# Attention and two expert stages on one core: the seven-product stage in four blocks of 384 tokens, TensorE operands placed by side of SBUF, begun at weight group 3

## The chip, the cores and the metric

The program runs on 1 core of one Trainium2 chip, and its other cores are idle. The metric is the device time of one execution in microseconds; a figure for the kernel is the median of its runs.

## The reference

The reference is a chain of three parts over B=2, H=8, S=768, D=64, that is 1,536 tokens of width 512. First comes windowed attention with block summaries, then a dense mixture of four experts (every expert works on every token), then a mixture of eight experts of which one or none is taken per token.

```python
x = attn_out.transpose(0, 2, 1, 3).reshape(B * S, H * D)   # 1536 x 512
p = domain_probs / (domain_probs.sum(-1, keepdims=True) + 1e-09)
for e in range(4):                                         # w1[e] 512x1024, w2[e] 1024x512
    h = np.maximum(x @ w1[e], 0.0)
    out += p[:, e:e + 1] * (h @ w2[e])
x = out
do_compute = x @ w_skip > 0
e_idx = argmax(x[do_compute] @ w_gate)                     # one of 8 experts
out[do_compute] = x + gate_w * (np.maximum(x @ w1[e], 0) @ w2[e])
```

The change touches the dense mixture above all. Its weights come in 16 groups: group g holds 256 of the 1,024 hidden columns of expert g // 4.

## The kernel before, in words

Every large product is made of three fp32r products of high and low parts: a value is copied to fp32r by ScalarE (`wh`, `xh`, `hh`), VectorE subtracts that from the value (`wl`, `xl`, `hl`), and TensorE forms h*h + h*l + l*h.

**Phase 1.** Groups 0 and 1 of the dense mixture run in blocks of two tiles (256 tokens) between the pieces of attention. As soon as attention is done, group 2 is loaded and split. **Plain groups.** Groups 2 and 3 run in `moe_block` with three blocks of 512 tokens. One chunk is half a group (128 hidden columns) for one block: `part_a` (line 363) makes 12 matmuls of 512 columns into one bank and then `hh` and `hl`; `part_b` (line 383) makes three matmuls of 512 columns per tile of 128 tokens with `w2`. In the order written out, the `part_b` of one chunk comes behind the `part_a` of the next.

**The seven-product stage.** `middle` takes groups 4 to 13. It multiplies `x` by `w1` of a group with seven products of half-size blocks in place of eight. The tokens are taken in pairs of blocks, here pair "l" (two blocks of 512 tokens) and pair "s" (two of 256). A product is a `burst` of six matmuls (line 509). Products 1, 2 and 3 use `x` itself, products 4 to 7 use sums of blocks of `x` (`xslh`, `xsll`, `xssh`, `xssl`), which `x_sums` makes once; products 3, 6 and 7 use sums of blocks of `w1` (`wsh`, `wsl`), which GpSimd makes per group (`sums`, lines 464 to 467) and ScalarE and VectorE split (`sum_parts`). Bursts accumulate in PSUM and are copied out between two of them: product 1 is copied from bank `ba` to `bb`, product 6 adds to `bb` and is copied out as `u2` (line 542), product 7 adds to `bb` and VectorE adds it to `s5` (line 551), product 4 adds to `bb` once more. `part` then makes `hh` and `hl` of a quarter of the hidden values. `second` (lines 570 and 572) multiplies them with `w2`, six matmuls of 512 columns for each tile, and VectorE adds the result into `acc`. A group has 42 burst matmuls of 512 columns, 42 of 256 and 72 of `second`. The order is a list (`order`), with one `second` after nearly every burst and the steps of the next group's weights (`w_steps`) at fixed places.

**Ends.** Groups 14 and 15 run in `moe_block` again, in blocks of 4, 3, 3 and 2 tiles, and the routing of each finished block (`route_block`) runs between the matmuls of the next one. The last block's routing runs beside the first slot ("x") of the routed mixture, whose rows are found from the first `NE` tiles alone. From `middle` on the order on every engine is as written; ahead of it a planner orders the instructions of each engine.

**Memory.** Tile pools grow from both ends of a partition. From the bottom: `ident`, `acc`, `pr`, `x` of tokens 512 to 1535, the buffers of `h`, the weight splits `w1`, `w2` of odd and even groups, `x` of tokens 0 to 511, the raw weights. From the top during `middle`: the pool `msum` (sums of `x`, sums of `w1`, `u2`, `s5`), and below it the pool `mh` (`hhl`, `hll`, `hhs`, `hls`). Added up from the tile sizes, all of the lower stack but the raw weights ends at byte 131,904, and `mh` and `msum` lie above byte 142,000.

Of the kernel before, what the change touches and what calls it, by code (L numbers as in the profile page):

```python
# [24 lines left out]
def attention_moe_kernel(  # L25
# [26 lines left out]
    acc = left.tile([P, NTILE, DM], F32, name="acc")  # L52
# [4 lines left out]
    xsplit = [None, [mp.tile([P, KC, NT - 4 * P], F32R, name=n) for n in ("xh1", "xl1")]]  # L57
# [5 lines left out]
    xsplit[0] = [xp.tile([P, KC, 4 * P], F32R, name=n) for n in ("xh0", "xl0")]  # L63
    wrp = xstack.enter_context(tc.tile_pool(name="wraw", bufs=1))

    def x_at(n0, n):

        i = int(n0 >= 4 * P)
        return [x[:, :, n0 - 4 * P * i : n0 - 4 * P * i + n] for x in xsplit[i]]


    wtiles = {}

    def w_parts(g, i):
        return [wps[g % 2].tile([P, KC * GF], F32R, name=f"w{i}{n}{g}", tag=f"w{i}{n}") for n in "hl"]

    def load_w(g):
        w1t = w_parts(g, 1)
# [13 lines left out]
        wtiles[g] = [raw, w1t, None]  # L92

    def split_w(g, i):
        if i > 1 and wtiles[g][2] is None:
            wtiles[g][2] = w_parts(g, 2)
        wh, wl = wtiles[g][1 + i // 2]
        w = KC * GF // 2
        s = slice(i % 2 * w, (i % 2 + 1) * w)
        r = wtiles[g][0][i // 2][:, s]  # L100
        (nc.gpsimd.tensor_copy if (g, i) in WPOOL else nc.scalar.copy)(wh[:, s], r)  # L101
        nc.vector.tensor_sub(wl[:, s], r, wh[:, s].bitcast(F32))  # L102
# [151 lines left out]
    def v_sum(b):  # L254
# [11 lines left out]
        vsum[b, "m"] = ap1.tile([WC, H * D + 8], F32, name=f"vsm{b}", tag="vsm")[:, : H * D]  # L266
# [77 lines left out]
    def moe_block(gs, t0, nt):  # L344
# [8 lines left out]
        def part_a(ci, c):  # L353
            g, cc = gs[ci // ncc], ci % ncc
            wh, wl = wtiles[g][1]
# [4 lines left out]
            f0 = c * GF + cc * P  # L360
# [6 lines left out]
            if c == KC - 1:  # L367
                hh = hp_.tile([P, 512], F32R, name=f"hh{g}_{t0}_{cc}", tag="hh")
                hl = hp_.tile([P, 512], F32R, name=f"hl{g}_{t0}_{cc}", tag="hl")
# [37 lines left out]
    SGROUPS = range(4, E1 * NG - 2)  # L407

    PAIRS = {"l": (4 * P, 4 * P), "s": (0, 2 * P)}
    xsum, scr = {}, {}  # L410

    def x_quarter(p, i, j, c=slice(0, 2)):

        n0, n = PAIRS[p]
        return [x[:, 2 * i + c.start : 2 * i + c.stop, :] for x in x_at(n0 + j * n, n)]

    def x_sums(pool):
# [3 lines left out]
        def unit(p, c):  # L421
            n = PAIRS[p][1]
            k = c.stop - c.start
            xt = {q: pool.tile([P, k, n], F32, name=f"x{q}{p}{c.start}", tag=f"x{q}") for q in ("11", "12", "21", "22")}
            ts = [pool.tile([P, k, n], F32, name=f"t{i}{p}{c.start}", tag=f"t{i}") for i in range(4)]
# [19 lines left out]
        for p, c in (("l", slice(0, 1)), ("l", slice(1, 2)), ("s", slice(0, 2))):  # L445
            us = []
            for i in range(12):
                def step(i=i, p=p, c=c, us=us):
                    if not us:
                        us.extend(unit(p, c))  # L450
                    us[i]()
                steps.append(step)
        return steps

    def w_steps(g):
# [3 lines left out]
        def sums():  # L459
            raw = wtiles[g][0][0].rearrange("p (c f) -> p c f", c=KC)  # L460
            a11, a12, a21, a22 = (raw[:, 2 * j : 2 * j + 2, i * P : (i + 1) * P] for i in range(2) for j in range(2))
            t = scr["w"].tile([P, 3, 2, P], F32, name=f"ws{g}", tag="ws")
# [5 lines left out]
            parts = [scr["w"].tile([P, 3, 2, P], F32R, name=f"ws{n}{g}", tag=f"ws{n}{g % 2}") for n in "hl"]  # L468
            wtiles[g] += [parts, t]

        def sum_parts(i):
            (h, l), t = wtiles[g][3:]
            s = slice(0, 2) if i == 0 else slice(2, 3)
            nc.scalar.copy(h[:, s], t[:, s])
            nc.vector.tensor_sub(l[:, s], t[:, s], h[:, s].bitcast(F32))  # L475
# [3 lines left out]
            lambda: load_w(g), sums if mid else no, lambda: split_w(g, 1), lambda: split_w(g, 0),  # L479
            (lambda: sum_parts(0)) if mid else no, (lambda: sum_parts(1)) if mid else no,  # L480
            lambda: split_w(g, 2), lambda: split_w(g, 3),
        ]

    def pair_work(g, p, state_):

        n0, n = PAIRS[p]
        w1h, w1l = wtiles[g][1]
        wsh, wsl = wtiles[g][3]
        e = g // NG
        ba, be, bb = (bank[i] for i in ((0, 6, 7) if p == "l" else (1, 6, 5)))  # L490
        hs, fs = {}, {}

        def wq(i, j):
            return [[w[:, (2 * j + c) * GF + i * P : (2 * j + c) * GF + (i + 1) * P] for w in (w1h, w1l)] for c in range(2)]

        def wsum(k):
            return [[w[:, k, c, :] for w in (wsh, wsl)] for c in range(2)]
# [16 lines left out]
        def tmp(nm):  # L514

            pad = 8 if nm + p == "s5s" else 0
            t = fs[nm] = scr["w"].tile([P, n + pad], F32, name=f"{nm}{p}{g}", tag=f"{nm}{p}")[:, :n]
            return t

        def part(i, j, src):  # L520
            if p == "l" and j == 1:
                pool, tag = hp_, ("hh", "hl")
            else:
                pool, tag = scr["h"], (f"hh{p}{i}{j}", f"hl{p}{i}{j}")
            hh, hl = (pool.tile([P, n], F32R, name=f"{t}_{p}{g}_{i}{j}", tag=t) for t in tag)
# [36 lines left out]
        def second(j, t):  # L562
            w2h, w2l = wtiles[g][2]
            b = bank[2 + state_["b"] % 3]
# [6 lines left out]
            t_ = n0 // P + j * (n // P) + t  # L571
# [7 lines left out]
    def middle(todo):  # L579

        todo = list(todo)
        state_ = dict(b=0)

        wh = wtiles[SGROUPS[0]][1][0]
        nc.tensor.matmul(bank[7], wh[:, :P], wh[:, :512], start=True, stop=True)
        at = {0: (0,), 2: (1,), 3: (2,), 5: (3,), 7: (4,), 9: (5,), 10: (6,), 12: (7,)}

        order = ("l1", "l5", "s1", "l6", "l3", "s6", "l7", "s5", "l2", "s7", "l4", "s3", "s2", "s4")
        for g in SGROUPS:
            nxt = w_steps(g + 1)  # L590
            work = {p: pair_work(g, p, state_) for p in PAIRS}
            for i, (p, k) in enumerate(order):
                work[p][0][k]()
                for k_ in at.get(i, ()):
                    nxt[k_]()
                if i == 10:
                    todo += work["l"][1][0]
                for _ in range(2 if g == SGROUPS[0] and i < 2 else i not in (9, 10)):
                    if todo:
                        todo.pop(0)()  # L600
            todo += work["l"][1][1] + work["s"][1][0] + work["s"][1][1]
        return todo
# [28 lines left out]
    NE = 7  # L631
# [650 lines left out]
    for g in range(2, SGROUPS[0]):  # L1282
        for i in range(3):
            moe_block((g,), 4 * i, 4)
    for gs, t0, n in (
        ((last - 1,), 0, 4), ((last,), 0, 4), ((last - 1,), 4, 3), ((last,), 4, 3),
        ((last - 1, last), 7, 3), ((last - 1, last), 10, 2),
    ):
        moe_block(gs, t0, n)
# [39 lines left out]
    for ch in chunks:  # L1329
# [13 lines left out]
        if ch["gs"] == (last - 1,) and first and ch["t0"] == 0:  # L1343
            ctx.enter_context(tc.manual_schedule())
            prev = dict(gs=(last - 2,), last=True, b=middle(prev["b"]))
            load_w(last)
        micros = list(ch["a"])
        if prev is not None:
            micros += prev["b"]
        for k_, f in enumerate(micros):  # L1350
# [6 lines left out]
            elif fin:  # L1357
                if ch["t0"] == 10 and ch["last"] and k_ == 1:
                    xt = slot_trans("x", early["xg"], bank[7])
                if ch["gs"] == (last - 1,) and ch["t0"] == 0 and k_ in (3, 6):  # L1360
                    split_w(last, 2 * ch["ci"] + k_ // 6)
                if ch["t0"] == 10 and ch["gs"][0] == last - 1 and micro_ % PRE == PRE - 1:
# [3 lines left out]
        if p1:  # L1366
            if ch["last"] and blk == len(PH1) - 1:
                run_to(len(alist))
                astack.close()
                scr["w"] = sstack.enter_context(tc.tile_pool(name="msum", bufs=1, side="right", reuse_waits="tile"))  # L1370
                for p_, (_, n_) in PAIRS.items():
                    xsum[p_] = [scr["w"].tile([P, 4, 2, n_], F32R, name=f"xs{p_}{q_}") for q_ in "hl"]
                xsteps = x_sums(tstack.enter_context(tc.tile_pool(name="mtmp", bufs=1, side="right", reuse_waits="tile")))
# [3 lines left out]
        elif not fin:  # L1377
# [7 lines left out]
            else:  # L1385
                if first and ch["t0"] == 0:
                    wsteps = w_steps(g + 1)
                for _ in range(1 + (len(wsteps) < 5)):
                    if wsteps:
                        wsteps.pop(0)()  # L1390
            for _ in range(3):
                xsteps.pop(0)()
            if not xsteps:
# [14 lines left out]
        if ch["gs"] == (last,) and ch["t0"] == 0 and ch["last"]:  # L1408
# [3 lines left out]
        if prev is not None and prev["gs"][-1] == last and prev["last"]:  # L1412
# [3 lines left out]
            if prev["t0"] == 4:  # L1416
                r += [None] * 3 + [early_list] + [None] * 3 + [early_gather, early_close]
            if prev["t0"] == 7:
# [45 lines left out]
    more_units(NTILE // 2 - 1, NTILE // 2)  # L1464
# [86 lines left out]
```

## Time and profile before

| | us |
|---|---|
| median of 3 runs | 700.65 |
| lowest and highest | 696.39 and 702.2 |
| the profiled execution | 699.05 |
| its span, first to last instruction | 697.3 |
| mean granted TensorE clock in it | 0.995 of full speed |

The profiled execution is 1.75 us longer than its span and 1.6 us shorter than the median. Times within a trace are counted from the start of the span. In a row of a group of instructions, "out<-in" names what is written and what is read; of a matmul the first name behind the arrow is the moving operand and the second the stationary one. Matmuls overlap in the records, so that the pace is read from start to start and not from the duration.

### The profile page before, as it was taken

The numbers are of one execution on the slowest core, as the hardware profiler recorded it, in microseconds if no ns is written. First come the engines' busy times: TensorE is split into PE (matmuls) and PEld (weight loads), VectorE is DVE, ScalarE is ACT, GpSimd is POOL, SyncE is SP. The second block draws the span as 40 slices with busy tenths as digits, with TensorE's granted clock in tenths as the row PEclk, the third lists the DMA queues.
The fourth block names the chain that finished last, engine by engine and source line by source line (L and its number), as shares of the span: only waits on it lengthen the run. The fifth ranks groups of instructions, "written<-read, shape, count | busy, mean of one in ns | idle before, by whom it ended". The sixth has DMA issues, their size and how long they took to land. (4 is left out here: it accounts for less than half of the span.)

```text
span 697.3 us, 10979 instructions
## 1 busy us (share of the span) xinstructions
PE 681.7 (98%) x4072; PEld 546.3 (78%) x4072; DVE 426.9 (61%) x1035; ACT 245.1 (35%) x617; POOL 103.4 (15%) x182
## 2 busy tenths in 40 slices
PE   6899999999999999999999999999999999999996
PEld 6788888788888888888888888888888888674361
DVE  5987664797537565665657465665653465694441
ACT  3766564432114232332323232232311223381250
POOL 5317200020101010101101010100010002331230
PEclk9999999999999999999999999999999999999999
DMA  8966210020000100000001100000050167668991
GB/s 240 258 208 162 65 47 24 31 91 31 31 0 31 61 31 31 31 31 30 31 31 37 54 31 31 31 31 30 31 213 0 62 259 300 211 221 317 413 410 53
DMA packets 39877, 73.78 MB, mean 106 GB/s; under 512 B 16740, under 2 KB 19812, under 8 KB 39824
## 3 DMA queue, kind: packets, MB, share of 16 engines
q1 hardware_dynamic: 38592, 70.31, 29.5%
q0 software_dynamic: 960, 2.25, 1.0%
q8 instruction: 32, 0.52, 0.3%
q10 hardware_dynamic: 272, 0.52, 0.2%
q14 instruction: 21, 0.17, 0.1%
HBM read 66.10 MB, written 7.86 MB: 106 GB/s over the span
## 5 line engine op out<-in xcount | busy, mean ns | idle before, releaser
L572 DVE SCALAR_TENSOR_TENSOR acc<-bank,pr,acc 128x512 f32<-128x512 f32 x120 | 89.4, 746 | 50.9 <-PE bank L570 50.2
L363 PE MATMUL bank<-xh,w1h 128*128 128x256 f32 (+2 forms) x208 | 68.5, 333 | 0.0
L363 PE MATMUL bank<-xl,w1h 128*128 128x256 f32 (+2 forms) x208 | 67.6, 326 | 0.0
L363 PE MATMUL bank<-xh,w1l 128*128 128x256 f32 (+2 forms) x208 | 67.4, 325 | 0.0
L383 PE MATMUL bank<-w2h,hh 128*128 128x512 f32 x144 | 58.4, 405 | 0.0
L464 POOL TENSOR_TENSOR ws<-raw 128x256 f32<-128x256 f32 x10 | 7.5, 750 | 332.6 <-DVE wsl L475 237.8
L383 PE MATMUL bank<-w2l,hh 128*128 128x512 f32 x144 | 56.5, 392 | 0.0
L370 ACT ACTIVATE hh<-bank 128x256 fp32r<-128x256 f32 (+2 forms) x52 | 24.1, 463 | 89.8 <-PE bank L363 83.5
L383 PE MATMUL bank<-w2h,hl 128*128 128x512 f32 x144 | 54.0, 398 | 1.6 <-DVE hl L371 1.6
L371 DVE SCALAR_TENSOR_TENSOR hl<-bank,hh 128x256 fp32r<-128x256 f32 (+2 forms) x52 | 27.0, 520 | 46.2 <-ACT hh L370 46.2
L295 ACT ACTIVATE sm<-sm,mn 128x120 f32<-128x120 f32 x96 | 36.7, 384 | 16.2 <-DVE mn L290 16.2
L363 PEld LDWEIGHTS bank<-xh,w1h 128*128 128x128 f32 x208 | 39.1, 189 | 4.2 <-DVE hl L371 0.4
L363 PEld LDWEIGHTS bank<-xl,w1h 128*128 128x128 f32 x208 | 39.4, 189 | 3.3
L363 PEld LDWEIGHTS bank<-xh,w1l 128*128 128x128 f32 x208 | 39.3, 189 | 2.5
L393 DVE SCALAR_TENSOR_TENSOR acc<-bank,pr,acc 128x512 f32<-128x512 f32 x43 | 29.8, 743 | 15.2 <-PE bank L383 15.2
L102 DVE TENSOR_TENSOR w1l<-raw,w1h 128x512 fp32r<-128x512 f32 x30 | 20.6, 690 | 22.4 <-ACT w1h L101 22.3
L383 PEld LDWEIGHTS bank<-w2h,hl 128*128 128x128 f32 x144 | 26.6, 188 | 8.7 <-DVE hl L371 3.3
L383 PEld LDWEIGHTS bank<-w2h,hh 128*128 128x128 f32 x144 | 27.2, 189 | 6.5 <-issue 2.3
L570 PE MATMUL bank<-w2h,hll_l 128*128 128x512 f32 x80 | 31.6, 395 | 0.0
L570 PE MATMUL bank<-w2l,hhl_l 128*128 128x512 f32 x80 | 31.6, 395 | 0.0
L570 PE MATMUL bank<-w2h,hhl_l 128*128 128x512 f32 x80 | 31.6, 395 | 0.0
L570 PE MATMUL bank<-w2h,hhs_s 128*128 128x512 f32 x80 | 31.6, 395 | 0.0
(357 smaller groups left out, 1741.1 us busy)
## 6 DMA issues: line engine op xcount, KB each, us to landing
raw<-in_moe_w_dram SPq DMA_DIRECT2D x30, 512.0 KB, 3.1
ra<-in_moe_w_dram SPq DMA_DIRECT2D x27, 512.0 KB, 9.8
rb<-in_moe_w_dram SPq DMA_DIRECT2D x21, 512.0 KB, 9.4
acc<-in_moe_w_dram SPq DMA_DIRECT2D x15, 512.0 KB, 10.1
vwin<-in_v_dram SPq DMA_DIRECT2D x24, 192.0 KB, 3.5
kt<-in_k_dram SPq DMA_DIRECT2D x8, 384.0 KB, 6.0
qbd<-in_q_dram SPq DMA_DIRECT2D x24, 128.0 KB, 4.0
out_dram<-xg SPq DMA_DIRECT2D x12, 256.0 KB, 3.0
```

The lines of the kernel that those rows point to most:

```text
L102: nc.vector.tensor_sub(wl[:, s], r, wh[:, s].bitcast(F32))
L295: nc.scalar.activation(sm[:, h, :], sm[:, h, :], AF.Exp, bias=mn[:, h : h + 1], scale=-1.0, accum_out=su[:, h : h + 1],)
L363: nc.tensor.matmul(b[:, :n], wt[:, f0 : f0 + P], xt[:, c, :], start=(c == 0 and i == 0), stop=(c == KC - 1 and i == 2),)
L370: nc.scalar.activation(hh[:, :n], b[:, :n], AF.Relu)
L371: nc.vector.scalar_tensor_tensor(out=hl[:, :n], in0=b[:, :n], scalar=0.0, in1=hh[:, :n].bitcast(F32), op0=ALU.max, op1=ALU.subtract,)
L383: nc.tensor.matmul(bank[2 + t], ht[:, t * P : (t + 1) * P], wt[:, f0 : f0 + DM], start=(ci == 0 and i == 0), stop=(ci == nch - 1 and i == 2),)
L393: nc.vector.scalar_tensor_tensor(out=a, in0=bank[2 + t], scalar=sc, in1=a, op0=ALU.mult, op1=ALU.add,)
L464: tt(out=t[:, 1], in0=a11, in1=a21, op=ALU.subtract)
L570: nc.tensor.matmul(b, a, w[:, s], start=i == 0 and k_ == 0, stop=i == 1 and k_ == 2)
L572: nc.vector.scalar_tensor_tensor(out=acc[:, t_, :], in0=b, scalar=pr[:, t_, e : e + 1], in1=acc[:, t_, :], op0=ALU.mult, op1=ALU.add,)
```

## The change

`acc` moves from the bottom of SBUF to its top. `x` is kept in two halves of 768 tokens. `w1` of a group is kept as two tiles, one for each half of the hidden columns. In the seven-product stage the second half of `w1` and two of the three sums of `w1` go to the upper pool `msum`, the third sum and the parts of two quarters of `h` to the pool `mh`, and the parts of the quarter (1, 1) to the room that the second half of `w1` leaves below. Added up from the tile sizes, the lower stack then ends at byte 113,472, `mh` lies between 113,600 and 129,984, and all operands of TensorE in `msum` lie above 133,000. Products 1, 2, 3 and `second` have both operands in the lower part, products 4 to 7 in the upper.

The pairs become "a" (tokens 0 to 767) and "b" (768 to 1535), each of two blocks of 384 tokens. The order of a group becomes: product 3 of the group before for a and b, load of the next weights, products 1a, 1b, the twelve `second` of the group before with most of the weight steps, 2a, 2b, 5a, 5b, 6a, 6b, 7a, 7b, 4a, 4b. The `hl` of a part is issued one step later than its `hh`. The stage begins at group 3. Group 2 and groups 14 and 15 run in blocks of three tiles, `NE` goes from 7 to 6, and the last block to be routed has three tiles in place of two. The sums of `x` start in the last block of phase 1, with the additions of high and low parts on GpSimd in place of VectorE.

```diff
-    acc = left.tile([P, NTILE, DM], F32, name="acc")
+    right = ctx.enter_context(tc.tile_pool(name="rows", bufs=1, side="right"))
+    acc = right.tile([P, NTILE * DM + 8], F32, name="acc")[:, : NTILE * DM].rearrange("p (t d) -> p t d", d=DM)
...
+    SGROUPS = range(3, E1 * NG - 2)
+    def w1_parts(g, i):
+        if i and g in SGROUPS:
+            return [scr["w"].tile([P, KC * P], F32R, name=f"w11{n}{g}", tag=f"w11{n}{g % 2}") for n in "hl"]
+        return [wps[g % 2].tile([P, KC * P], F32R, name=f"w1{i}{n}{g}", tag=f"w1{i}{n}") for n in "hl"]
...
-    PAIRS = {"l": (4 * P, 4 * P), "s": (0, 2 * P)}
+    TB = 3 * P
+    PAIRS = {"a": 0, "b": 2 * TB}
...
             def whole(i, j):
                 h, l = x_quarter(p, i, j, c)
-                nc.vector.tensor_add(xt[f"{i + 1}{j + 1}"], h.bitcast(F32), l.bitcast(F32))
+                nc.gpsimd.tensor_tensor(out=xt[f"{i + 1}{j + 1}"], in0=h.bitcast(F32), in1=l.bitcast(F32), op=ALU.add)
...
+            pool, s = (scr["w"], slice(0, 2)) if i == 0 else (scr["h"], slice(2, 3))
...
-        ba, be, bb = (bank[i] for i in ((0, 6, 7) if p == "l" else (1, 6, 5)))
+        ba, be, bb = (bank[i] for i in ((0, 4, 6) if p == "a" else (1, 5, 7)))
...
             nc.scalar.activation(hh, src, AF.Relu)
-            nc.vector.scalar_tensor_tensor(
+            state_["late"].append(lambda: nc.vector.scalar_tensor_tensor(
                 out=hl, in0=src, scalar=0.0, in1=hh.bitcast(F32), op0=ALU.max, op1=ALU.subtract,
-            )
+            ))
...
-            b = bank[2 + state_["b"] % 3]
+            b = bank[2 + state_["b"] % 4]
...
-        order = ("l1", "l5", "s1", "l6", "l3", "s6", "l7", "s5", "l2", "s7", "l4", "s3", "s2", "s4")
+        x = x_at(0, 4 * P)[0][:, 0, :]
+        for b in (bank[6], bank[7]):
+            nc.tensor.matmul(b, x[:, :P], x, start=True, stop=True)
+        def step(f):
+            late, state_["late"] = state_["late"], []
+            f()
+            for l in late:
+                l()
+        work = None
         for g in SGROUPS:
+            last_, work = work, {p: pair_work(g, p, state_) for p in PAIRS}
             nxt = w_steps(g + 1)
+            if last_:
+                step(last_["a"][0]["3"])
+                step(last_["b"][0]["3"])
+            nxt[0]()
+            step(work["a"][0]["1"])
+            step(work["b"][0]["1"])
+            if last_:
+                todo += [f for j in range(2) for p in PAIRS for f in last_[p][1][j]]
+            at = {1: 1, 2: 2, 5: 3, 7: 4, 9: 7}
+            for i, f in enumerate(todo):
+                step(f)
+                if i in at:
+                    nxt[at.pop(i)]()
+            for k in at.values():
+                nxt[k]()
+            todo = []
+            step(work["a"][0]["2"])
+            step(work["b"][0]["2"])
+            nxt[5]()
+            step(work["a"][0]["5"])
+            step(work["b"][0]["5"])
+            nxt[6]()
+            for k in "674":
+                for p in PAIRS:
+                    step(work[p][0][k])
...
-    NE = 7
+    NE = 6
...
-        for i in range(3):
-            moe_block((g,), 4 * i, 4)
+        for i in range(4):
+            moe_block((g,), 3 * i, 3)
-    for gs, t0, n in (
-        ((last - 1,), 0, 4), ((last,), 0, 4), ((last - 1,), 4, 3), ((last,), 4, 3),
-        ((last - 1, last), 7, 3), ((last - 1, last), 10, 2),
+    for gs, t0 in (
+        ((last - 1,), 0), ((last,), 0), ((last - 1,), 3), ((last,), 3), ((last - 1, last), 6), ((last - 1, last), 9),
     ):
```

## Rows read from the trace of the kernel before

**Rows 1.** The page, busy time of TensorE, its share of the span, instructions

```profile
PE 681.7 (98%) x4072; PEld 546.3 (78%) x4072; DVE 426.9 (61%) x1035; ACT 245.1 (35%) x617; POOL 103.4 (15%) x182
```

**Rows 2.** The waits of TensorE's matmuls: us in total, times, longest

```profile
PE bank L383 <- DVE hl L371: 1.6, 3, 0.9
```

**Rows 3.** Busy time by stretch, core 0: the plain groups, one seven-product group

```profile
139.18:205.11 65.93, 65.92 (x289) 53.91 (x288) 43.63 (x68) 16.25 (x29) 6.64 (x8) 1.00 0.11 40
...
246.00:277.35 31.35, 31.35 (x158) 26.40 (x157) 19.28 (x31) 9.66 (x20) 3.28 (x4) 1.00 0.10 34
```

**Rows 4.** TensorE in order of time, behind the stage: start, duration

```profile
533.89 0.39 PE L363 MATMUL bank<-xh,w1h 128*128 128x512 f32 x1
...
539.33 0.33 PE L363 MATMUL bank<-xh,w1h 128*128 128x384 f32 x1
...
541.43 0.39 PE L383 MATMUL bank<-w2h,hh 128*128 128x512 f32 x1
...
544.19 0.33 PE L363 MATMUL bank<-xh,w1h 128*128 128x384 f32 x1
...
573.94 0.33 PE L363 MATMUL bank<-xh,w1l 128*128 128x384 f32 x1
...
575.50 0.34 PE L363 MATMUL bank<-xh,w1l 128*128 128x384 f32 x1
```

**Rows 5.** TensorE in order of time, within the seven-product stage

```profile
380.94 0.39 PE L570 MATMUL bank<-w2h,hh_l 128*128 128x512 f32 x1
...
382.34 0.39 PE L509 MATMUL bank<-xh,w1h 128*128 128x512 f32 x1
...
383.71 0.39 PE L570 MATMUL bank<-w2h,hh_l 128*128 128x512 f32 x1
...
385.07 0.40 PE L509 MATMUL bank<-xslh,w1h 128*128 128x512 f32 x1
...
517.43 0.39 PE L570 MATMUL bank<-w2h,hhs_s 128*128 128x512 f32 x1
...
523.00 0.39 PE L363 MATMUL bank<-xh,w1h 128*128 128x512 f32 x1
```

**Rows 6.** The groups of instructions: busy us, mean ns | idle before

```profile
L101 ACT CAST w2h<-raw 128x512 fp32r<-128x512 f32 x29 | 17.4, 614 | 4.7 <-PE bank L383 3.8 <-DMA raw<-in_moe_w_dram 1.0
...
L466 POOL TENSOR_TENSOR ws<-raw 128x256 f32<-128x256 f32 x10 | 10.0, 1000 | 0.8
...
L464 POOL TENSOR_TENSOR ws<-raw 128x256 f32<-128x256 f32 x10 | 7.5, 750 | 332.6 <-DVE wsl L475 237.8 <-DMA raw<-in_moe_w_dram 94.8
```

**Rows 7.** Lines 542, 551, 527: duration ns min/median/max, first and last start

```profile
L542 ACT COPY u2l<-bank x10: 586/586/587, 211.8 to 485.6; 128x512 f32<-128x512 f32 x10
L542 ACT COPY u2s<-bank x10: 357/372/372, 214.8 to 490.6; 128x256 f32<-128x256 f32 x10
...
L551 DVE TENSOR_TENSOR s5l<-bank,s5l x10: 683/691/692, 216.3 to 493.3; 128x512 f32<-128x512 f32 x10
L551 DVE TENSOR_TENSOR s5s<-bank,s5s x10: 418/424/425, 219.8 to 500.3; 128x256 f32<-128x256 f32 x10
...
L527 DVE SCALAR_TENSOR_TENSOR hls_s<-u2s,hhs_s x10: 424/870/878, 223.6 to 504.4; 128x256 fp32r<-128x256 f32 x10
```

**Rows 8.** All engines in order of time at the end of a product 7

```profile
367.44 0.39 PE L509 MATMUL bank<-xslh,wsl 128*128 128x512 f32 x1
...
367.86 0.69 DVE L551 TENSOR_TENSOR s5l<-bank,s5l 128x512 f32<-128x512 f32 x1 [0.42 <-PE bank L509]
```

**Rows 9.** Busy time by stretch while the sums of x are made

```profile
128.00:163.00 35.00, 33.95 (x168) 27.69 (x168) 35.00 (x59) 15.45 (x30) 3.69 (x4) 1.00 0.17 61
```

**Rows 10.** In order of time, the last routing and the first gather behind it

```profile
610.53 0.22 DVE L749 CUSTOM_DVE_ANT_0 jk<-bank,oh,nin 128x8 f32<-128x8 f32 x1
...
612.67 1.04 POOL L1016 DMA_INDIRECT xg<-out_dram,ixb  x1 [1.79 <-DVE ixb L817]
...
616.18 0.61 PE L1030 MATMUL bank<-ident,xg 128*128 128x128 f32 x4
```

More of the change, by code (lines that the diff above doesn't have):

```diff
@@ L91, in load_w @@
         )
-        wtiles[g] = [raw, w1t, None]
+        wtiles[g] = [raw, [None, None], None]
     def split_w(g, i):
[L95 to L102, printed above, removed]
+        cp = nc.gpsimd.tensor_copy if (g, i) in WPOOL else nc.scalar.copy
+        if i < 2:
+            h, l = wtiles[g][1][i] = w1_parts(g, i)
+            r = wtiles[g][0][0].rearrange("p (c f) -> p c f", c=KC)[:, :, i * P : (i + 1) * P]
+            h, l = (t.rearrange("p (c f) -> p c f", c=KC) for t in (h, l))
+        else:
+            if wtiles[g][2] is None:
+                wtiles[g][2] = [wps[g % 2].tile([P, KC * GF], F32R, name=f"w2{n}{g}", tag=f"w2{n}") for n in "hl"]
+            sl = slice((i - 2) * DM, (i - 1) * DM)
+            h, l = (t[:, sl] for t in wtiles[g][2])
+            r = wtiles[g][0][1][:, sl]
+        cp(h, r)
+        nc.vector.tensor_sub(l, r, h.bitcast(F32))
     astack = ExitStack()
@@ L402, in moe_block @@
             ))
[L407 to L410 removed]
+    TB = 3 * P
+    PAIRS = {"a": 0, "b": 2 * TB}
     def x_quarter(p, i, j, c=slice(0, 2)):
[L414 to L415 removed]
+        return [x[:, 2 * i + c.start : 2 * i + c.stop, :] for x in x_at(PAIRS[p] + j * TB, TB)]
     def x_sums(pool):
@@ L443, in unit, with step @@
             ]
[L445 to L452, printed above, removed]
+        for p in PAIRS:
+            for c in (slice(0, 1), slice(1, 2)):
+                us = []
+                for i in range(12):
+                    def step(i=i, p=p, c=c, us=us):
+                        if not us:
+                            us.extend(unit(p, c))
+                        us[i]()
+                    steps.append(step)
         return steps
@@ L581, in middle @@
         todo = list(todo)
[L582 to L586, printed above, removed]
-        order = ("l1", "l5", "s1", "l6", "l3", "s6", "l7", "s5", "l2", "s7", "l4", "s3", "s2", "s4")
+        state_ = dict(b=0, late=[])
+        x = x_at(0, 4 * P)[0][:, 0, :]
+        for b in (bank[6], bank[7]):
+            nc.tensor.matmul(b, x[:, :P], x, start=True, stop=True)
@@ new lines, in middle @@
+            for k in at.values():
[8 more added lines that the diff above has]
+            for k in "674":
+                for p in PAIRS:
+                    step(work[p][0][k])
+        step(work["a"][0]["3"])
+        step(work["b"][0]["3"])
+        step(lambda: None)
+        return [f for j in range(2) for p in PAIRS for f in work[p][1][j]]
@@ L1346, in attention_moe_kernel @@
             load_w(last)
+        if p1 and first and blk == len(PH1) - 1:
+            run_to(len(alist))
+            astack.close()
+            scr["w"] = sstack.enter_context(tc.tile_pool(name="msum", bufs=1, side="right", reuse_waits="tile"))
+            scr["t"] = scr["w"].tile([P, 3, 2, P], F32, name="ws")
+            for p_ in PAIRS:
+                xsum[p_] = [scr["w"].tile([P, 4, 2, TB], F32R, name=f"xs{p_}{q_}") for q_ in "hl"]
+            xsteps = x_sums(tstack.enter_context(tc.tile_pool(name="mtmp", bufs=1, side="right", reuse_waits="tile")))
         micros = list(ch["a"])
@@ L1366, in attention_moe_kernel @@
         if p1:
+            if blk == len(PH1) - 1:
+                for _ in range(3):
+                    xsteps.pop(0)()
             if ch["last"] and blk == len(PH1) - 1:
[L1368 to L1373, printed above, removed]
                 load_w(2)
@@ L1387, in attention_moe_kernel @@
                     wsteps = w_steps(g + 1)
[L1388 to L1391, printed above, removed]
+                if wsteps:
+                    wsteps.pop(0)()
+            for _ in range(min(len(xsteps), 6)):
                 xsteps.pop(0)()
-            if not xsteps:
+            if not xsteps and "h" not in scr:
                 tstack.close()
@@ L1407, in attention_moe_kernel @@
                 free += [rap.tile([P, FF], F32, name=f"ra{i}") for i in range(NRA)]
-        if ch["gs"] == (last,) and ch["t0"] == 0 and ch["last"]:
+        if ch["gs"] == (last,) and ch["t0"] == 3 and ch["last"]:
             xstack.close()
```

104 lines of the change are left out of this document (46 added, 58 removed).

## The prediction

> **What bounds the kernel now.** I read the page first: TensorE is busy for 681.7 of 697.3 us [rows 1]. Then its waits: of the dense mixture only 1.6 us in three waits for an `hl` are left [rows 2]. The view by stretch says the same of the part that changes: in a seven-product group TensorE is busy for 31.35 of 31.35 us, VectorE for 19.28, ScalarE for 9.66, GpSimd for 3.28, at a granted clock of 1.00, the 2.4 GHz level [rows 3]. Nothing waits there, so the time is the number of matmuls times their pace, and the reader has to look at the pace from start to start. Behind the stage, where weights and moving operand both lie in the lower stack, 24 matmuls of 512 columns go from 533.89 to 539.33, 226.7 ns each, and nine of 384 go from 573.94 to 575.50, 173.3 ns each [rows 4]. Within the stage the pace depends on what is multiplied. A `second` with `hh_l` (lower stack) and `w2`, behind a product 1 of 512 columns, takes from 383.71 to 385.07 for its six, 226.7 ns each; but 24 matmuls of `second` with `hhs_s`, `hls_s` (above) and `w2` (below) go from 517.43 to 523.00, 232.1 ns each [rows 5]. So there is some 5 ns on a matmul of 512 columns whose operands lie on two sides. By the layout those are 18 burst matmuls and 48 of `second` in each group.
>
> **The change part by part.**
>
> *The ten groups 4 to 13.* A group keeps its 84 burst matmuls and 72 of `second`, and its burst columns: 42 x (512 + 256) = 84 x 384. With both operands on one side everywhere, as the sizes give it, a group is 84 x 173.3 + 72 x 226.7 ns = 14.56 + 16.32 = 30.88 us. To that come changes of size. Behind a change the pace is off for a while: twelve matmuls of 384 took 2.10 us in place of 2.08, the twelve of 512 behind them 2.76 in place of 2.72 [rows 4]; that is 0.06 us for there and back, once per group. A change of side at 384 columns is in no row; I bound it by nothing and by that 0.04 each and take 0.02, twice: 30.98 us. Against 31.35 that is 0.37 less, **3.7 us** for ten groups; with no cost of a change 4.7, with none of the gain 0.
>
> What hides the other engines' work there: copies and parts run while TensorE does the other pair's burst, 6 x 173.3 = 1.04 us. VectorE's addition began 0.42 us after the start of the last matmul of a product 7 [rows 8], some 0.2 after that matmul's share of 0.23 was over. At 384 columns it takes some 0.56 us and a copy by ScalarE 0.48 (between the rows for 256 and 512, [rows 7]), so a bank is free 0.7 to 0.76 us after its burst and wanted after 1.04. No wait, with 0.3 us to spare; without that cover each of four handovers (6 to 7 and 7 to 4, a and b) would cost what is missing. VectorE, ScalarE and GpSimd keep the amounts of [rows 3], far from the 31 us. I take nothing.
>
> *Group 3.* The two plain groups fill 65.93 us, 32.97 each [rows 3]; 32.97 to 30.98 is **2.0 us** less (1.6 at the old pace).
>
> *Entry of the stage.* In its first group only the last three `part_b` (9 x 226.7 = 2.04 us) stand where later twelve `second` do, and all weight steps of group 4 come at once, ahead of the Relus on ScalarE. With time counted from the start of 1a: two dummy matmuls and 1a, 1b end at 2.5, the copy of 1b at 3.2, the cast of `w1` at 3.8 (0.61 [rows 6]), its subtraction on VectorE at 4.5, GpSimd's four operations (0.75 to 1.0 each [rows 6], some 3.3) at 7.8. Then ScalarE has two casts of the sums, two Relus, two casts of `w2`, two copies of `s5` and that of `u2a`, 0.4 to 0.6 each, until about 12.2. TensorE wants to begin 7a at 2.5 + 2.04 + 6 x 1.04 = 10.8. I take a wait of **1.4 us**, once; 0 if the planner brings the weights earlier, 3 if GpSimd is slow. The second dummy is **0.2**. Behind TensorE nothing else is queued.
>
> *Group 2 and the ends.* Group 2 in four blocks is 96 x 173.3 + 72 x 226.7 = 32.96 us plus eight times 0.06, 33.4 against 32.97: **0.5 us** more. In groups 14 and 15 the columns and the count (192 of `part_a`) stay; four to eight chunks more change size: **0.3 us**.
>
> *The last routing.* The first gather starts at 612.67 and its rows are transposed at 616.18 [rows 10], 3.5 us later; I take it that TensorE has no slack there. With a third tile VectorE's chain of small operations ahead of the gather is longer by about a microsecond (an estimate: some six operations for each tile at the 0.22 us of one of them, [rows 10]), and TensorE's own steps for that tile, moved here from an earlier block, cover half: **0.5 us**, 0 to 1.5. The loads of the routed weights start a block of three tiles earlier and one 512 KB unit of `acc` comes free later; TensorE waits for none of them now. Nothing.
>
> *The sums of `x`.* VectorE is full from 128 to 163 us [rows 9], with 36 steps of x at about 0.69 [rows 7] among others; in 384 columns and without the additions it has 32 of about 0.56, 7 us less. They are needed some 30 us earlier than now, at the first 5a near 180 us, and GpSimd is idle there but for 6.64 us in 65.93 [rows 3]. Against that, VectorE has to wait for GpSimd's 16 additions of about 1 us. I take 0, from 1 us better (the waits of [rows 2] lie here) to 6 worse.
>
> *Sum.* -3.7 - 2.0 + 1.4 + 0.2 + 0.5 + 0.3 + 0.5 = -2.8 us, 699.05 to 696.25 for the profiled execution, which lies 1.6 under the median: **697.9 us** as a median. The three runs of before lie 5.8 us apart, and I count 1% (7 us) as what a measurement here can tell from no change.
>
> **The rivals.**
>
> *The side doesn't matter* (the change doesn't do what it says). The 5 ns could come from the alternation with bursts of 256 columns. For it speaks that a `second` with both operands below also takes 1.40 us between two bursts of 256 (380.94 to 382.34, [rows 5]); against it, that the 24 mixed ones in a row never come back to 226.7. Then eleven groups stay at 31.35 and the sum is -1.6 + 2.9 = +1.3: 702.0 us. The Trainium skill speaks for this rival: by "TensorE: Matmul & The Clock Gate", Part 2, step 1, TensorE reads moving operand and weights through two independent ports, and loading the next weights takes nothing from the running matmul. By that rule the time is this rival's; the 232.1 against 226.7 ns do not agree with it.
>
> *Slower: the sums of `x` come late.* Place: group 2, where VectorE's queue holds `total` and `low` behind GpSimd's additions and the `hl` of `part_a` behind those; `part_b` then waits for `hl`, as it did in [rows 2]. For it: a VectorE subtraction with two inputs in SBUF took 0.87 us in the median against 0.42 at its shortest [rows 7], where GpSimd was at work on the sums of `w1`. If each of the 16 additions costs VectorE as much as it takes, 16 us are added to a stretch that ends with some 10 to spare, and about 6 us of waits are left: 697.9 + 6 = 704. It decides from 2.8 us of such waits on, where the gain is gone. Against it: VectorE has 7 us less to do, and the planner may place the `hl` first. The Trainium skill, "SBUF — State Buffer", "Who interferes with whom", states that a VectorE instruction with two SBUF inputs contends with a GpSimd instruction that reads SBUF; the 0.87 us agree.
>
> *Slower: the handover of the banks is too tight.* If copy or addition is 0.2 us over its 0.3 of slack, four waits in eleven groups give 8.8 us: 706.7. Against it stand [rows 8].
>
> *More than forecast.* No changes of pace to pay (4.7 and 2.1), no entry and no last routing to pay, and the waits of [rows 2] gone: -4.7 - 2.1 - 1.0 + 1.0 = -6.8, 693.9 us.
>
> **How the numbers follow.** Forecast 0.55, side without effect 0.17, late sums 0.11, handover 0.07, more than forecast 0.10. The forecast's own terms go from 696 to 700; the range that leaves out 2 in 10 takes in the side rival and the late sums: 694 to 705 us. Faster by over 1% (under 693.6) is most of the last case with the spread of runs, 0.11; slower by over 1% (over 707.7) the far ends of the two slow rivals, 0.08; within 1% 0.81.
>
> **What would show it.** Right: in the profile after, a group of 31.0 us, 24 matmuls of `second` in 5.44 us with `h` of any quarter, twelve of 384 in 2.08 with sums of `x`; one wait of about 1.4 us of TensorE near the first 7a; TensorE's waits for `hl` no longer than now. Wrong: `second` at 232 ns, idle TensorE in every group ahead of 7 or 4, or waits for `hl` between 140 and 180 us.

## The result, and the profile after

After: **707.06 us** (median of 10 runs, 703.87 to 710.56) against 699.73 for before on the same chips (10 runs, 695.36 to 702.2). The ratio is 1.0108, 95% interval 1.0080 to 1.0137: the change costs 7.3 us. The profiled execution took 707.03 us with a span of 705.3, against a span of 697.3 before. Much of the spread between runs arises in phase 1, ahead of the stages in question (two runs below, alike up to there but for 128 unused bytes, begin the first `part_a` of group 2 at 139.61 and 145.18 us), so I read the stages, not the whole.

The page of after, the line that answers to [rows 1]:

```profile
PE 682.3 (97%) x4107; PEld 572.1 (81%) x4107; DVE 432.5 (61%) x1041; ACT 250.7 (36%) x633; POOL 125.2 (18%) x202
```

TensorE is busy for 0.6 us more than before, in a span that is 8.0 us longer: the loss is idle time. Its waits (us in total, times, longest), to be held against [rows 2]:

```profile
PE bank L396 <- DVE hl L384: 8.4, 4, 4.7
```

The three waits of before for `hl` came to 1.6 us, the four of after come to 8.4. Where they lie and what else happens there, by stretch (us, then busy time and instructions of TensorE, weight loads, VectorE, ScalarE, GpSimd, the granted clock, DMA share, GB/s):

```profile
128.00:164.00 36.00, 27.59 (x146) 23.88 (x145) 35.74 (x48) 14.79 (x31) 21.81 (x19) 0.95 0.17 59
144.00:148.00 4.00, 0.14 (x1) 0.00 (x0) 4.00 (x6) 1.98 (x4) 2.96 (x3) 1.00 0.36 131
148.00:152.00 4.00, 3.14 (x10) 2.94 (x11) 4.00 (x6) 2.11 (x5) 3.51 (x4) 0.57 0.00 0
229.70:260.90 31.20, 31.20 (x157) 28.17 (x157) 18.79 (x31) 9.67 (x21) 3.01 (x4) 1.00 0.10 34
```

The first line answers to [rows 9]. VectorE is full in both, but in after it finishes 48 instructions in 36 us, in before 59 in 35 us, and GpSimd is busy for 21.81 us in place of 3.69. TensorE stands for almost all of 144 to 148. In the next four microseconds the granted clock is 0.57, that is partly the 1.2 GHz level, after an idle time of 4.7 us:

```profile
148.86 1.22 PE L396 MATMUL bank<-w2h,hl 128*128 128x512 f32 x2 [4.72 <-DVE hl L384]
...
151.17 0.52 PE L376 MATMUL bank<-xl,w11h 128*128 128x384 f32 x1
...
152.13 0.33 PE L376 MATMUL bank<-xh,w11l 128*128 128x384 f32 x1
```

Two matmuls of 512 columns and eight of 384 take 3.27 us from start to start, where 226.7 and 173.3 ns each make 1.84: the clock costs some 1.4 us more. The last line of the stretches is one seven-product group: 31.20 us, where [rows 3] has 31.35 and the prediction 30.98.

The wait of 4.7 us ends with the `hl` at 148.40. VectorE in order of time ahead of it (start, duration):

```profile
142.50 2.63 DVE L115 TENSOR_TENSOR w2l<-raw,w2h 128x512 fp32r<-128x512 f32 x2
145.06 1.07 DVE L445 TENSOR_TENSOR xsal<-t2a,xsah 128x384 fp32r<-128x384 f32 x1
146.05 0.55 DVE L441 TENSOR_TENSOR t3a<-x21a,t1a 128x384 f32<-128x384 f32 x1
146.52 0.68 DVE L115 TENSOR_TENSOR w10l<-raw,w10h 128x512 fp32r<-128x512 f32 x1
147.12 1.35 DVE L441 TENSOR_TENSOR t0b<-x12b,x11b 128x384 f32<-128x384 f32 x1
148.40 0.41 DVE L384 SCALAR_TENSOR_TENSOR hl<-bank,hh 128x256 fp32r<-128x256 f32 x1
```

and GpSimd in the same time:

```profile
142.12 1.33 POOL L438 TENSOR_TENSOR x22b<-xh,xl 128x384 f32<-128x384 f32 x1
143.41 1.17 POOL L475 TENSOR_TENSOR raw<-raw 128x256 f32<-128x256 f32 x1
144.66 1.05 POOL L476 TENSOR_TENSOR ws<-raw 128x256 f32<-128x256 f32 x1
146.68 1.38 POOL L438 TENSOR_TENSOR x21b<-xh,xl 128x384 f32<-128x384 f32 x1 [0.96 <-DVE t3a L441]
```

The same kind of VectorE subtraction takes 0.55 us at 146.05, where GpSimd has nothing to do, and 1.35 us at 147.12, with `x21b` running on GpSimd. ScalarE had written the `hh` that this `hl` needs by 141.35; the `hl` stood in VectorE's queue behind sums of x and splits of weights. How far these were stretched, from the groups of VectorE's instructions between 128 and 172 us (busy us, mean ns):

```profile
L115 DVE TENSOR_TENSOR w2l<-raw,w2h 128x512 fp32r<-128x512 f32 x4 | 5.0, 1289 | 0.0
...
L445 DVE TENSOR_TENSOR xsal<-t3a,xsah 128x384 fp32r<-128x384 f32 x2 | 2.7, 1368 | 0.0
L441 DVE TENSOR_TENSOR t1a<-x22a,t0a 128x384 f32<-128x384 f32 x2 | 2.7, 1346 | 0.0
L115 DVE TENSOR_TENSOR w11l<-raw,w11h 128x512 fp32r<-128x512 f32 x2 | 2.2, 1092 | 0.0
...
L441 DVE TENSOR_TENSOR t2a<-x22a,x12a 128x384 f32<-128x384 f32 x2 | 1.1, 548 | 0.0
```

The last line is the undisturbed price at 384 columns; at 512 it is 0.68 (the `w10l` above). The ten operations of the first four lines lose 6.5 us by that. Over all of VectorE's operations with both operands in SBUF between attention and the stage, the loss adds up to 11.7 us, in before to 1.1. The 17 of 384 columns that had no GpSimd instruction beside them took 0.54 to 0.56 us, twelve of the 15 that had one 0.65 to 1.38. The `hl`, with one operand in PSUM, took 0.41 and 0.55 us whether GpSimd worked or not. VectorE is busy for 35.74 of 36 us there, so the loss is not time in which it stands and waits for GpSimd's sums.

The other finding is in the pace. One run of `second` in after, TensorE in order of time:

```profile
387.79 0.39 PE L586 MATMUL bank<-w2h,hh_a 128*128 128x512 f32 x1
...
390.55 0.39 PE L586 MATMUL bank<-w2h,hh_a 128*128 128x512 f32 x1
...
395.99 0.40 PE L586 MATMUL bank<-w2h,hha 128*128 128x512 f32 x1
...
404.36 0.33 PE L520 MATMUL bank<-xh,w10h 128*128 128x384 f32 x1
```

The first twelve take 2.76 us, as [rows 4] had it behind a change of size. The next 24 take 5.44, 226.7 ns each. The last 36, with `hha` to `hlb` as weights, take 8.37 us, 232.5 ns each, though these tiles lie at 117,696 to 129,472 and `w2` at 56,128 to 78,656: both below byte 131072. The side of SBUF is not what decides. Nor is it the place of one operand alone: with both operands in the upper stack a product of six took 1.04 us, 173.3 ns each, as with both in the lower, and two products with `x` below and `ws1` above took 2.11, some 176 ns each:

```profile
377.35 0.33 PE L520 MATMUL bank<-xsah,ws0h 128*128 128x384 f32 x1
...
378.39 0.33 PE L520 MATMUL bank<-xsbh,ws0h 128*128 128x384 f32 x1
...
383.59 0.34 PE L520 MATMUL bank<-xh,ws1h 128*128 128x384 f32 x1
...
385.70 0.34 PE L520 MATMUL bank<-xh,w10h 128*128 128x384 f32 x1
```

### The profile page after: what moved, and what is told of

It reads as the page before. It is cut to its first block, busy times and chain, and to the rows that moved or that the text cites. A ratio compares the mean times of both kernels' runs of the same rounds, so it can differ in the third digit from the quotient of the medians.

```text
span 705.3 us, 11110 instructions
## 1 busy us (share of the span) xinstructions
PE 682.3 (97%) x4107; PEld 572.1 (81%) x4107; DVE 432.5 (61%) x1041; ACT 250.7 (36%) x633; POOL 125.2 (18%) x202
## 5 line engine op out<-in xcount | busy, mean ns | idle before, releaser
L376 PE MATMUL bank<-xh,w11h 128*128 128x256 f32 (+1 forms) x96 | 31.3, 326 | 0.0
L292 PE MATMUL bank<-kw,qbd 128*128 128x120 f32 x192 | 27.2, 292 | 3.6 <-DVE kw L233 2.6
L376 PE MATMUL bank<-xl,w11h 128*128 128x256 f32 (+1 forms) x96 | 30.4, 316 | 0.0
L376 PE MATMUL bank<-xh,w11l 128*128 128x256 f32 (+1 forms) x96 | 30.2, 315 | 0.0
L376 PE MATMUL bank<-xh,w10h 128*128 128x256 f32 (+1 forms) x96 | 30.2, 314 | 0.0
L376 PE MATMUL bank<-xl,w10h 128*128 128x256 f32 (+1 forms) x96 | 29.8, 310 | 0.0
L376 PE MATMUL bank<-xh,w10l 128*128 128x256 f32 (+1 forms) x96 | 29.7, 309 | 0.0
L520 PE MATMUL bank<-xh,w10l 128*128 128x384 f32 x88 | 29.6, 336 | 0.0
L520 PE MATMUL bank<-xh,w10h 128*128 128x384 f32 x88 | 29.5, 336 | 0.0
L520 PE MATMUL bank<-xl,w10h 128*128 128x384 f32 x88 | 29.5, 335 | 0.0
```

Source lines behind the costliest of these rows:

```text
L292: nc.tensor.matmul(ps[:, h * WC : (h + 1) * WC], qb[b, t // 2][:, t % 2, h, :], kwin[b, t // 4][:, t % 4, h, :], start=True, stop=True,)
L376: nc.tensor.matmul(b[:, :n], wt[:, f0 : f0 + P], xt[:, c, :], start=(c == 0 and i == 0), stop=(c == KC - 1 and i == 2),)
L520: nc.tensor.matmul(b[:, :n], w[c][a], x[c][m], start=start and c == 0 and i == 0, stop=c == 1 and i == 2, skip_group_check=True,)
```

## The experiments

Two questions. **Why is `hl` late?** Theory *contention*: GpSimd's additions and VectorE's operations with two operands in SBUF hold each other up. Rival *density*: the sums are squeezed into a shorter time, whoever does them. **What sets 226.7 or 232 ns?** Theory *phase*: added up from the tile sizes, the operands in the lower stack begin at 320 modulo 512 bytes and those in the upper one at 448, in before and after alike; a pair is slow if its two addresses differ by 128, whatever half they lie in. Rival: a boundary at some address.

**The upper stack 128 bytes lower, in after.**

```
-acc = right.tile([P, NTILE * DM + 8], F32, name="acc")...
+acc = right.tile([P, NTILE * DM + 40], F32, name="acc")...
```

> After with the first tile of the upper stack (acc) 128 bytes longer, so that every tile of that stack lies 128 bytes lower; nothing else changes. Theory (phase): what slows a matmul is not the half of SBUF but that weights and moving operand differ by 128 modulo 512 bytes. In after all lower tiles have 320 modulo 512 and all upper ones 448, and the 36 `second` per group whose h lies in the upper stack run at 232.3 ns where the other 36 run at 226.7. With the shift both stacks have 320: those 36 go to 226.7, the twelve matmuls with ws1 from 176 to 173.3, a group from 31.20 to 30.96 us, eleven groups save 2.6: 704.4 us. Rival (a boundary at an address, at 131072 or elsewhere): 128 bytes move no tile across one, `second` stays at 232.3, a group at 31.20, 707.0 us.

704.25 us (ratio to before 1.0097, 1.0071 to 1.0124), 2.8 under after as medians; by the ratios, whose intervals overlap, the gain is smaller, so the stage itself has to show it. One group, and the run of `second` that answers to 395.99 to 404.36 above:

```profile
321.14:352.08 30.94, 30.94 (x157) 28.09 (x157) 18.82 (x31) 9.66 (x21) 3.01 (x4) 1.00 0.11 34
```

```profile
362.36 0.39 PE L586 MATMUL bank<-w2h,hha 128*128 128x512 f32 x1
...
370.52 0.33 PE L520 MATMUL bank<-xh,w10h 128*128 128x384 f32 x1
```

36 matmuls in 8.16 us, 226.7 ns each; the group is at 30.94, 0.04 under the prediction's 30.98. Phase holds; a boundary at some address would have left these 36 where they were.

**The same shift in before.**

```
 acc = left.tile([P, NTILE, DM], F32, name="acc")
+right = ctx.enter_context(tc.tile_pool(name="rows", bufs=1, side="right"))
+right.tile([P, 32], F32, name="shift")
```

> Before with a tile of 128 bytes at the top of the upper stack, so that all its tiles lie 128 bytes lower; nothing else changes. Theory phase: in before the 48 `second` and 36 burst matmuls per group that take one operand from each stack differ by 128 modulo 512 bytes; all come to 226.7 at 512 columns, a group goes from 31.35 to 30.95 us, ten groups save 4: 695.7 us. Rival (half of SBUF, as predicted): every pair lies on the same two sides as before, 232 ns stay, 31.35, 699.7 us.

695.07 us, ratio 0.9954 (0.9932 to 0.9976), with no operand on another side than before. A group, and the 24 matmuls that took 5.57 us in [rows 5]:

```profile
255.34:286.36 31.02, 31.02 (x158) 26.42 (x156) 19.27 (x31) 9.66 (x20) 3.28 (x4) 1.00 0.11 35
```

```profile
513.02 0.39 PE L572 MATMUL bank<-w2h,hhs_s 128*128 128x512 f32 x1
...
518.46 0.39 PE L365 MATMUL bank<-xh,w1h 128*128 128x512 f32 x1
```

5.44 us, 226.7 ns. The group of 31.35 [rows 3] is at 31.02: the gain that the change sought, for 128 unused bytes.

**Which modulus.** The same tile in before with 384 bytes, then with 64.

```
-right.tile([P, 32], F32, name="shift")
+right.tile([P, 96], F32, name="shift")    # second run: [P, 16]
```

> Before with a tile of 384 bytes at the top of the upper stack in place of 128: weights and moving operand of a pair from both stacks differ by 256 modulo 512 bytes and by 0 modulo 256. If what must agree is the address modulo 256, the mixed pairs run at 226.7, group 31.0, about 695 us; if it is modulo 512, they stay at 232, 31.3 to 31.35, about 699 us.

> Before with a tile of 64 bytes there: mixed pairs differ by 64 modulo 128 bytes, where before they differ by 128. By the phase theory they stay off 226.7, at 232 or slower, group 31.3 or longer, 699 us or more; by a boundary at an address nothing changes against before.

One run each: 695.98 and 701.04 us. A group of the first, then of the second:

```profile
442.56:473.58 31.02, 31.02 (x158) 26.42 (x157) 19.00 (x32) 9.78 (x20) 0.00 (x0) 1.00 0.11 36
```

```profile
446.80:478.18 31.38, 31.38 (x157) 26.37 (x156) 18.97 (x32) 9.78 (x20) 0.00 (x0) 1.00 0.11 36
```

A difference of 256 is as good as none (31.02 in both); differences of 64 and 128 are slow (31.38, and 31.35 before). Of the four differences tried, 0 and 256 are fast: what has to agree here is the address modulo 256 bytes.

**The additions on VectorE again, in after.**

```
-nc.gpsimd.tensor_tensor(out=xt[...], in0=h.bitcast(F32), in1=l.bitcast(F32), op=ALU.add)
+nc.vector.tensor_add(xt[...], h.bitcast(F32), l.bitcast(F32))
```

> After with the 16 additions `whole` back on VectorE. Theory contention: GpSimd's additions stretch VectorE's subtractions beside them from 0.55 to 1.3 us, some 11.6 us in all between 128 and 172; without them TensorE's waits for hl fall from 8.4 us to 3 or less, 701 us. Theory density: 48 steps in twelve chunks, 30 us earlier than before, are too much for VectorE whoever adds; the 16 additions cost it 16 x 0.55 = 8.8 us and give back 8 to 11 of contention, the waits for hl stay between 6 and 10 us, 705 to 708 us.

703.10 us (1.0070, 1.0040 to 1.0101): 4 us better than after, between what the two theories said. The waits, and the durations of line 474 (minimum, median, maximum in ns, first and last start):

```profile
PE bank L396 <- ACT hh L383: 4.3, 1, 4.3
PE bank L396 <- DVE hl L384: 0.8, 1, 0.8
```

```profile
L474 POOL TENSOR_TENSOR ws<-raw x11: 734/737/5473, 140.1 to 430.3; 128x256 f32<-128x256 f32 x11
```

The waits for `hl` are down to 0.8 us, but a new one came, for `hh`. The first sum of `w1` for group 3 took 5.47 us on GpSimd, seven times its median, beside VectorE's additions and subtractions in close order; ScalarE's cast of `w11`, which needs those sums, waited, and the Relu stood behind the cast. Contention again, with GpSimd the one that is held up.

**Group 3's sums of `w1` on VectorE as well.**

```
-tt = nc.gpsimd.tensor_tensor
+tt = nc.vector.tensor_tensor if g == SGROUPS[0] else nc.gpsimd.tensor_tensor
```

> After with the 16 additions `whole` and group 3's four sums of w1 on VectorE, so that GpSimd does nothing beside VectorE until group 4's sums. In the run with `whole` alone on VectorE one wait of 4.3 us was left: a sum of w1 on GpSimd took 5.47 us beside back-to-back subtractions of VectorE, ScalarE's casts waited for it and the Relu stood behind them. Theory contention (GpSimd and VectorE hold each other up whenever VectorE reads two operands in SBUF, in both directions): the waits of TensorE between 130 and 165 fall to 1.5 us or less although VectorE has 1.7 us more to do; 698 to 699.5 us. Theory density (the same work in 30 us less): VectorE is full all the same, 3 us or more of waits stay, at another hl; 701.5 us or more.

699.75 us (1.0023, 0.9999 to 1.0046), 7.3 under after as medians. Waits, and the stretch that answers to the first one of after:

```profile
PE bank L396 <- DVE hl L384: 2.7, 3, 1.0
PE bank L376 <- DVE hl L384: 0.2, 1, 0.2
```

```profile
128.00:164.00 36.00, 33.04 (x180) 28.93 (x179) 35.66 (x71) 15.91 (x34) 3.42 (x3) 1.00 0.17 60
```

VectorE has twenty additions more than in after, and in the same 36 us it finishes 71 instructions in place of 48. TensorE's waits fall from 8.4 to 3.0 us and the granted clock stays at 1.00. The expected time was missed by a quarter of a microsecond, since 3.0 us of waits stayed, not 1.5.

**The additions on GpSimd, in before.** The one part of the change alone; the edit of the first run on additions, the other way round.

> Before with its twelve additions `whole` (128x512) on GpSimd and nothing else changed: the one part of the change alone. Theory contention: VectorE is relieved of 12 x 0.68 = 8.2 us and loses 8 to 12 to stretched operations, GpSimd's additions and the sums of w1 take 1.3 us and more, and what waits for them on ScalarE and VectorE stands ahead of Relu and hl; TensorE's waits between 130 and 180 us grow from 1.0 to 4 us or more, 702 to 704 us. Theory density: the sixteen chunks are there as before and VectorE has 8 us less to do; the waits stay at 1 us or less, 698.5 to 699 us.

703.91 us, 1.0080 (1.0053 to 1.0107): 5.1 over before, with twelve additions moved to an engine that had little to do there.

```profile
PE bank L383 <- DVE hl L371: 6.4, 5, 2.6
PE bank L363 <- DVE hl L371: 0.6, 1, 0.6
```

```profile
128.00:164.00 36.00, 30.05 (x162) 24.02 (x161) 32.91 (x41) 15.03 (x29) 19.06 (x14) 1.00 0.18 59
```

7.0 us of waits in the whole run in place of 1.6, at the old density; VectorE's operations with two operands in SBUF lose 9.6 us. Density alone said 1 us of waits or less.

**More time for the sums.** Seven products from group 4 on, no steps in phase 1:

```
-SGROUPS = range(3, E1 * NG - 2)
+SGROUPS = range(4, E1 * NG - 2)
-            if blk == len(PH1) - 1:
-                for _ in range(3):
-                    xsteps.pop(0)()
...
-            for _ in range(min(len(xsteps), 6)):
+            for _ in range(min(len(xsteps), 4 if len(xsteps) > 36 else 3)):
```

> After with the seven products from group 4 on (group 3 plain, in four blocks of 384), no sums in phase 1 and 3 or 4 steps of the sums per chunk over fifteen of the sixteen chunks of groups 2 and 3; the additions stay on GpSimd. Theory density: the waits for hl go to 2 us or less, group 3 costs 1.8 more: 707.0 - 9.2 + 1.8 = 699.6 us. Theory contention: VectorE's operations are still stretched by the same 11 us in a stretch in which it was full in before too, and 3 to 5 us of waits stay: 702 to 705 us.

707.39 us (1.0130, 1.0092 to 1.0169): worse than either theory said.

```profile
PE bank L396 <- DVE hl L384: 3.4, 4, 1.5
PE bank L396 <- ACT hh L383: 1.8, 1, 1.8
PE bank L376 <- DVE hl L384: 1.4, 1, 1.4
```

6.6 us of waits stayed. A step that is issued later in the program doesn't run later here: the first `t0a` starts at 130.91, still in phase 1, where the planner has put it. So this run gave the sums no more time, and tells nothing of density. With the additions on VectorE too:

> After with the seven products from group 4 on, the steps of the sums over fifteen chunks and none in phase 1, and additions and the first group's sums of w1 on VectorE. By contention as the larger and density as the smaller cause: with neither, TensorE's waits between 130 and 180 us are 1.2 us or less in place of the 3.0 that stayed with all additions on VectorE; group 3 costs 1.8 more: about 699.5 us. If density has no part, 3 us of waits stay here too: 701.5 us.

699.01 us (one run).

```profile
PE bank L396 <- DVE hl L384: 2.1, 3, 0.8
PE bank L376 <- DVE hl L384: 0.3, 1, 0.3
```

2.4 us of waits against 3.0: neither 1.2 nor 3. No operation of VectorE is stretched in this run, so what is left of the waits is not contention; where it comes from is open.

**Both causes removed.** All first additions on VectorE and the stack shifted:

> The same with the upper stack 128 bytes lower. The two causes don't touch each other, so the gain of 2.8 us that the shift gave alone is added: 695.2 to 696.7 us by theory contention, 698.7 or more by theory density.

697.91 us (0.9977, 0.9952 to 1.0002), 1.8 under the run without the shift, 1.2 above the top of the expected span; the two medians are uncertain by about as much. A group takes 30.94 us here too. A step further, with four products of rows and routing weight on ScalarE:

```
+if gs[0] == 0 and t0 >= 8:
+    nc.scalar.activation(a, bank[2 + t], AF.Copy, scale=sc)
```

> After with all additions of the first sums on VectorE, the upper stack 128 bytes lower, and the four first products of rows times routing weight of the last two blocks of phase 1 on ScalarE in place of VectorE (4 x 0.74 us). If VectorE's load is what is left of the waits, they fall from 3.0 to about 1 us: 695.5 to 696.5 us; if not, 697.9.

696.95 us (0.9972, 0.9951 to 0.9993). The waits are at 2.7 us (2.4 for `hl`, 0.3 for `hh`), so VectorE's load is not what is left of them. Both kernels are beaten, but before with 128 unused bytes (695.07) isn't.

**The two causes side by side.** Phase 1 ends, for this count, with attention's last matmul that reads `pt`; the stage begins with its first burst. Counted from these two starts in each trace, the spread of phase 1 drops out. "Lost" is what VectorE's operations with two operands in SBUF took over their undisturbed price in that time (all in us):

| run | lost | attention to stage | stage to end |
|---|---|---|---|
| before | 1.1 | 75.9 | 495.3 |
| before, 128 bytes lower | 1.1 | 75.9 | 492.4 |
| before, 384 bytes lower | 1.2 | 75.9 | 492.4 |
| before, 64 bytes lower | 1.1 | 75.9 | 495.8 |
| before, additions on GpSimd | 9.6 | 82.0 | 495.7 |
| after | 11.7 | 53.3 | 525.6 |
| after, 128 bytes lower | 11.6 | 53.3 | 522.5 |
| after, additions on VectorE | 2.7 | 49.5 | 525.0 |
| after, group 3's sums too | 1.2 | 46.7 | 525.1 |
| both causes removed | 1.2 | 46.6 | 522.6 |
| and four products on ScalarE | 0.2 | 46.2 | 522.5 |
| after, stage from group 4 | 10.1 | 85.5 | 494.3 |
| the same, all on VectorE | 0.0 | 79.1 | 494.2 |

In before and in the last two runs the stage begins at group 4, in the other runs of after at group 3. Where GpSimd works moves the one column and leaves the other (495.7 and 525.1) within 0.6 us; the shift moves the other by 2.5 to 3.1 and leaves the one within 0.1.

## Why the prediction was wrong

It said 697.9 us and slower only if two rivals went far. Step by step:

*The sums of `x`: the step that failed.* "I take 0, from 1 us better to 6 worse." TensorE's waits for `hl` between 130 and 165 us went from 1.0 (1.6 less one of 0.6 near 600 us) to 8.4 us, three times the 2.8 from which the rival decides, and the clock cost about 1.4 more. Taking GpSimd out of this stretch gave back 6.7 us between attention and the stage. The mechanism stood in the text as a rival, with the right place, the right queue and the right row: a subtraction at 0.87 us against 0.42 [rows 7]. Its chance was 0.11 because "VectorE has 7 us less to do". That count gave the remaining operations their undisturbed price, against its own row of 0.87 us. The additions took 1.0 to 1.45 us each on GpSimd, and beside them and the sums of `w1` VectorE's operations lost 11.7 us. VectorE's queue got slower by moving work off it. The rival's price of 6 us was too small, too (7.4 of waits and 1.4 of clock came): it let ten microseconds of room at the end of the stretch absorb the first ten, but `part_b` waits for each `hl` as it comes, and the 4.7 us at 144 were lost long before that end. "The planner may place the `hl` first" didn't come true: `hl` at 148.40 stands behind sums.

The Trainium skill, "SBUF — State Buffer", "Who interferes with whom", says that a VectorE instruction with two SBUF inputs contends with a GpSimd instruction that reads SBUF, and that the order of issue decides who blocks. The runs agree in both directions: 0.55 against 1.35 us on VectorE in after, where `x21b` had begun on GpSimd 0.44 us earlier, and 0.74 against 5.47 on GpSimd with the additions on VectorE, where VectorE was already at work. The prediction named the first half and still put the cost at 0.

*The ten groups, the second step that failed: -3.7 predicted, -1.5 measured* (31.35 to 31.20, ten times). The price of a slow pair, 5.4 ns, was right; the reason was not. All pairs of [rows 5] that lie on two sides also lie in two stacks, and the stacks' operands differ by 128 bytes modulo 256. The change put the sums of x and their weights together, but left 36 `second` (8.37 us in place of 8.16) and twelve burst matmuls with `ws1` to pairs from both stacks. 0.21 of the 0.26 us that separate 31.20 from 30.94 are those `second`. The rival "the side doesn't matter" was right as a sentence and wrong as a time: it gave 31.35, since it knew no other cause.

The Trainium skill's rule behind that rival, in "TensorE: Matmul & The Clock Gate", Part 2, step 1, is that loading the next weights takes nothing from the running matmul. Read that way, no pace would depend on where the weights lie. The 128-byte shift, which changes nothing else, takes 232.5 to 226.7 ns; the measurement decides.

*Right:* 0.06 us per group for changes of size (twelve `second` behind a burst 2.76 us, as predicted); the handover of the banks, where no wait stands in the middle of the stage; the pace of 384 columns.

*Too dear:* the entry wait of 1.4 us didn't come, since TensorE has no wait over 0.1 us between 160.20 and 518 us. Nor did the 0.5 of the last routing: TensorE has no wait of its own there, only 0.2 us for `rxt`, as the list of its waits shows.

```profile
PE bank L740 <- ACT rxt L741: 0.2, 1, 0.2
```

*The rest of the span's 8.0 us.* Attention to stage: before needs 75.9 us to group 4, that is 42.9 without a plain group of 32.97; after needs 53.3, which is 10.4 more. Of these 7.4 are waits and 1.4 the clock; 0.7 only moved (three matmuls of `part_b` more stand ahead of the stage), and 0.9 stay for group 2 (+0.5 predicted), the dummies (+0.2) and what isn't told apart. Group 3 saves 1.8 (32.97 to 31.20), not 2.0. From the first `part_a` of group 14 to the transposition of [rows 10], without the `second` between, before takes 95.9 us and after 96.1: 0.15 more, where the ends and the last routing were put at 0.8. About 1.5 us remain, in phase 1 (0.3), the first and last of the eleven groups (0.7) and behind the routing (0.5), of which no run tells the reason.

## What to carry to other kernels

An idle engine is not free if its work slows the full one: before moving an addition to GpSimd, count what VectorE does beside it with two SBUF operands at about double its time (here ten operations at 12.8 us in place of 6.3), and who waits behind it in VectorE's queue. A correlation in the rows (slow pairs lie on two sides) needs a second variable ruled out before a layout is rebuilt on it: here a shift of 128 bytes, which no code notices, told the two apart and gave more than the rebuilt layout. A step issued later in the program need not run later where a planner orders the queue (here 130.9 us against 129.6). And where runs differ by several microseconds ahead of the change, count between two events of the program, not over the whole.

## What the runs showed of the hardware that was not expected

The pace of back-to-back fp32r matmuls depends in these runs on the addresses of weights and moving operand modulo 256 bytes: 226.7 ns for 512 columns where they agree, 231 to 234 where they differ by 64 or 128. In the shifted after every product ran at 226.7 or 173.3 ns but for the first two of 512 and the first of 384 columns behind a change of size. The 24 matmuls of [rows 5] that take 5.57 us in before and 5.44 with a difference of 0 take 5.44 us with one of 256 and 5.60 with one of 64, here in this order:

```profile
514.12 0.39 PE L572 MATMUL bank<-w2h,hhs_s 128*128 128x512 f32 x1
...
519.56 0.39 PE L365 MATMUL bank<-xh,w1h 128*128 128x512 f32 x1
```

```profile
519.25 0.40 PE L572 MATMUL bank<-w2h,hhs_s 128*128 128x512 f32 x1
...
524.85 0.39 PE L365 MATMUL bank<-xh,w1h 128*128 128x512 f32 x1
```

Why the chip behaves so, no run here shows.
